# The last expert's mask of remaining rows in the second mixture's search: made and read in PSUM instead of SBUF

## The chip, the core and the metric

The kernel runs on one core of one Trainium2 chip. The metric is the device time of one execution in microseconds (us), the median over several runs. TensorE (PE) multiplies matrices out of SBUF into PSUM; VectorE (DVE), ScalarE (ACT) and GpSimd (POOL) do elementwise work; SyncE (SP) issues most DMAs. Each engine runs its own instructions in order and waits on semaphores of the others. DVE and ACT reach SBUF and PSUM, POOL reaches SBUF.

## What is computed

Causal attention with a decay (4 batches, 8 heads, 576 positions, 64 wide) gives 2304 rows of 512. Two mixtures of experts follow. The change lies in the second, whose reference is:

```python
def _moe2_ref(x, w_gate, w1, w2):
    N, D = x.shape                 # 2304, 512
    E = w_gate.shape[1]            # 8
    cap = N // E                   # 288
    logits = x @ w_gate
    order = np.argsort(-logits.flatten())
    assigned = -np.ones(N, dtype=np.int64)
    counts = np.zeros(E, dtype=np.int64)
    for idx in order:
        tok, e = (int(idx) // E, int(idx) % E)
        if assigned[tok] >= 0 or counts[e] >= cap:
            continue
        assigned[tok] = e
        counts[e] += 1
    out = np.zeros((N, D), dtype=np.float32)
    for e in range(E):
        mask = assigned == e
        out[mask] = np.maximum(x[mask] @ w1[e], 0.0) @ w2[e]
    return out
```

Row after row takes the best expert that still has room; every expert ends with 288 rows.

## The kernel before

**The second mixture** (`Moe2Quick`) fills one expert after the other, in phases 0 to 7. For each phase `search` finds the expert and the threshold, `hand` makes the mask `m` of that expert's rows (tile `mem`) and reads the expert's number to SP, which can then fetch its weights; `listing` turns the mask into row numbers (two groups of matmuls, L1927 to L1929 and the 21 of L1954, with DVE work between) and gathers the rows with three indirect DMAs on POOL; `prep` transposes the gathered rows; and `FFN.run` does the expert's two layers. Rows are kept 128 to a partition, 18 columns (`NT`); `V` holds the 8 logits of each row (18 x 8 on the free axis), large negative where the row or the expert is closed.

**The last phase (ph = 7) has no threshold.** All rows not yet taken belong to it. In `search` (L1804 to L1811) `es` becomes a mask of the one open expert, L1807 takes the maximum of each row's 8 logits, L1808 turns it into 1 (row open) or 0, and `hand` uses this mask as `new`: L1903 and L1905 find the rows whose first choice is that expert among those of earlier phases, and L1907 adds `new`. The mask is a tile `v` of the SBUF pool `p`. The other phases keep such small results in PSUM: `open` (L1775 to L1778) takes one bank for the search and names its columns:

```python
S, G = self.S, self.G = [self.ps.tile([128, 512], F32, name=n) for n in ("sq", "gq")]
self.base, self.u, self.g = S[:, 96:128], S[:, 128:128 + NT], S[:, 152:152 + NT]
self.hg = S[:, 208:208 + NT * E].rearrange("p (t e) -> p t e", e=E)
```

so that `u`, the maximum of each row, is 18 columns of the tile that the profile calls `sq`. Phases 1 to 6 write it at L1814; nothing reads it after phase 6.

**An expert's two layers.** `FFN.run` makes 8 groups (f = 0 to 7) of 12 matmuls at L733: four pieces of the contraction, three products each, since every factor is split into a rounded part (`xh`, `wh`) and a rest (`xl`, `wl`). A group's result lies in one of four PSUM tiles `ph`. ACT writes its rounded positive part (`hh`, L761; `h`, L764), and DVE the rest of it (`hl`, L737, called `low`). Only after `low` is the PSUM tile free, so group f needs `low` of group f - 4, or of a tile used before. `by_row` (L799, L806) does the second layer. The weights come in 8 pieces of 512 KB per expert: SP issues the DMA into `wraw` (L685, L689), ACT rounds it into `wh` (L699), POOL subtracts into `wl` (L703, 128 x 1024). POOL also issues the gathers (L1968) and, three per expert, the scatters of finished rows (L2037).

**The order of the work.** A schedule is built as the program is written: generators ("lanes" for search, listing, prep and out) yield the time at which a model of the engines (`pace`) expects their next step to be ready, and are woven between the matmuls of `run`. Each engine then keeps that order. So DVE has the `low` of groups 1 and 2 behind the whole of `hand(7)`.

Of the kernel before, what the change touches and what calls it, by code (L numbers as in the profile page):

```python
# [7 lines left out]
F32 = mybir.dt.float32  # L8
# [4 lines left out]
ALU = mybir.AluOpType  # L13
AX = mybir.AxisListType
# [1259 lines left out]
class Moe2:  # L1274
# [7 lines left out]
    NT = N // 128  # L1282
# [343 lines left out]
class Moe2Quick(Moe2):  # L1626
# [158 lines left out]
    def search(self):  # L1785

        nc, p, NT, rt, pace = self.nc, self.p, self.NT, self.rt, self.f.pace
        V, rem, S, es, u, g, acc, base = self.V, self.rem, self.S, self.es, self.u, self.g, self.acc, self.base
# [12 lines left out]
        for ph in range(E):  # L1801
            while ph > self.cur + 2:
                yield pace.t + 1.0
            if ph == E - 1:  # L1804
                nc.vector.tensor_scalar(es, rem, 1e8, None, op0=ALU.is_lt)
                op = p.tile([128, NT], F32, name="v")
                nc.vector.tensor_reduce(op, V, axis=AX.X, op=ALU.max)  # L1807
                nc.vector.tensor_scalar(op, op, -1.0, None, op0=ALU.is_gt)  # L1808
                pace.dve(0.8)
                self.hand(ph, es, op)  # L1810
                return  # L1811
            hb, thr = self.hb0, self.thr
            if ph:
# [6 lines left out]
                                               op0=ALU.mult, op1=ALU.add, accum_out=room)  # L1820
# [382 lines left out]
```

## Time and profile before

| | |
|---|---|
| Runs of the kernel | median 766.86 us of 3 (765.68 to 766.95) |
| The profiled execution | 765.09 us, of which 763.4 us from the first to the last instruction (the span) |
| PE busy | 692.2 us (91%), granted clock 0.952 on average |
| DVE, ACT, POOL busy | 349.1 us (46%), 393.8 us (52%), 488.2 us (64%) |
| Second mixture, expert phase 4: first L733 to the next expert's | 629.71 to 660.71 us |
| The same, phase 5 | 660.71 to 698.01 us |

Times in views are us from the span's start. A row of a timeline gives start, duration, engine, line, operation, the tile written and those read, their shapes, and in brackets how long the engine sat idle before and what released it. The granted clock is the share of TensorE's full speed (2.4 GHz) that the chip's throttle let through, so 0.50 is 1.2 GHz. DVE's instructions in a timeline may overlap a little, because the next one starts while the last one drains; the step from start to start is then the better measure.

### The profile page before, as it was taken

The numbers are of one execution on the slowest core, as the hardware profiler recorded it, in microseconds if no ns is written. First come the engines' busy times: TensorE is split into PE (matmuls) and PEld (weight loads), VectorE is DVE, ScalarE is ACT, GpSimd is POOL, SyncE is SP. The second block draws the span as 40 slices with busy tenths as digits, with TensorE's granted clock in tenths as the row PEclk, the third lists the DMA queues.
The fourth block names the chain that finished last, engine by engine and source line by source line (L and its number), as shares of the span: only waits on it lengthen the run. The fifth ranks groups of instructions, "written<-read, shape, count | busy, mean of one in ns | idle before, by whom it ended". The sixth has DMA issues, their size and how long they took to land. (4 is left out here: it accounts for less than half of the span.)

```text
span 763.4 us, 16041 instructions
## 1 busy us (share of the span) xinstructions
PE 692.2 (91%) x5723; PEld 576.1 (75%) x5723; DVE 349.1 (46%) x1307; ACT 393.8 (52%) x924; POOL 488.2 (64%) x524
## 2 busy tenths in 40 slices
PE   6999999999529999999999998399999999979994
PEld 3566565665329999999999987287878989868893
DVE  4776675866622222232232243655636646472120
ACT  5988788787115455455555551143533535434440
POOL 6666338170248676777777872359779788768861
PEclk9999999999759999999999999579999999989997
DMA  6588556220168272743835800347527366268201
GB/s 199 170 315 304 187 177 215 86 102 2 63 216 286 84 253 75 268 157 138 294 117 178 279 33 28 91 166 252 190 94 248 125 195 210 90 214 278 62 34 39
DMA packets 79395, 124.32 MB, mean 163 GB/s; under 512 B 10989, under 2 KB 43757, under 8 KB 79296
## 3 DMA queue, kind: packets, MB, share of 16 engines
q1 hardware_dynamic: 72944, 103.80, 41.4%
q0 software_dynamic: 6160, 18.97, 6.8%
q8 instruction: 49, 0.80, 0.4%
q14 instruction: 50, 0.41, 0.2%
q10 hardware_dynamic: 192, 0.34, 0.1%
HBM read 101.08 MB, written 22.18 MB: 161 GB/s over the span
## 5 line engine op out<-in xcount | busy, mean ns | idle before, releaser
L703 POOL TENSOR_TENSOR wl<-wraw,wh 128x1024 fp32r<-128x1024 f32 x128 | 305.4, 2397 | 100.2 <-ACT wh L699 94.7
L733 PE MATMUL ph<-xh,wh 128*128 128x288 f32 (+6 forms) x512 | 162.8, 318 | 5.7 <-DVE hl L737 4.3
L733 PE MATMUL ph<-xl,wh 128*128 128x288 f32 (+6 forms) x512 | 155.3, 303 | 0.6 <-DVE xl L2004 0.3
L699 ACT CAST wh<-wraw 128x1024 fp32r<-128x1024 f32 x128 | 132.7, 1050 | 44.6 <-DMA wraw<-in_moe_w_dram 31.7
L733 PE MATMUL ph<-xh,wl 128*128 128x288 f32 (+6 forms) x512 | 154.5, 302 | 0.0
L761 ACT ACTIVATE hh<-ph 128x256 fp32r<-128x256 f32 (+6 forms) x128 | 51.5, 402 | 112.7 <-PE ph L733 107.4
L733 PEld LDWEIGHTS ph<-xh,wh 128*128 128x128 f32 x512 | 99.2, 194 | 10.7 <-issue 8.0
L733 PEld LDWEIGHTS ph<-xl,wh 128*128 128x128 f32 x512 | 99.2, 194 | 2.0 <-DVE xl L2004 1.8
L737 DVE SCALAR_TENSOR_TENSOR hl<-ph,hh 128x256 fp32r<-128x256 f32 (+6 forms) x128 | 55.6, 442 | 96.5 <-ACT hh L761 55.8
L733 PEld LDWEIGHTS ph<-xh,wl 128*128 128x128 f32 x512 | 98.8, 193 | 0.2 <-POOL wl L703 0.2
L174 ACT ACTIVATE z<-z,mx 128x128 f32<-128x128 f32 (+2 forms) x144 | 84.0, 584 | 27.1 <-DVE mx L177 25.2
L177 DVE CUSTOM_DVE_ANT_0 z<-ps,cx 128x128 f32<-128x128 f32 (+2 forms) x144 | 68.6, 518 | 51.0 <-PE ps L188 33.5
L733 PE MATMUL ph<-hh,wh 128*128 128x288 f32 (+6 forms) x256 | 79.4, 310 | 0.0
L733 PE MATMUL ph<-hh,wl 128*128 128x288 f32 (+6 forms) x256 | 76.8, 300 | 0.9 <-POOL wl L703 0.8
L733 PE MATMUL ph<-hl,wh 128*128 128x288 f32 (+6 forms) x256 | 76.7, 300 | 0.0
L151 POOL TENSOR_SCALAR_AFFINE_SELECT cx<-cb 128x256 f32<-128x256 f32 (+1 forms) x64 | 44.5, 726 | 38.9 <-DVE mx L177 16.9
L208 ACT COPY pt<-tp 128x512 f32<-128x512 f32 (+2 forms) x128 | 49.9, 438 | 7.3 <-PE tp L216 5.8
L799 PE MATMUL ph<-wh,hh 128*128 128x512 f32 x128 | 53.6, 419 | 0.0
L799 PE MATMUL ph<-wh,hl 128*128 128x512 f32 x128 | 50.6, 395 | 0.0
L216 PEld LDWEIGHTS tp<-ident,z 128*128 128x128 f32 x320 | 34.7, 140 | 20.7 <-ACT z L174 6.9
L799 PE MATMUL ph<-wl,hh 128*128 128x512 f32 x128 | 50.3, 393 | 0.0
L733 PEld LDWEIGHTS ph<-hh,wl 128*128 128x128 f32 x256 | 48.3, 189 | 1.4 <-POOL wl L703 1.4
(353 smaller groups left out, 1192.2 us busy)
## 6 DMA issues: line engine op xcount, KB each, us to landing
wraw<-in_moe_w_dram SPq DMA_DIRECT2D x128, 512.0 KB
cb<-c8d SPq DMA_DIRECT2D x15, 576.0 KB
xs<-zrow SPq DMA_DIRECT2D x8, 803.1 KB
xg<-xs SPq DMA_DIRECT2D x6, 771.0 KB
kd<-in_k_dram SPq DMA_DIRECT2D x16, 288.0 KB
qd<-in_q_dram SPq DMA_DIRECT2D x16, 288.0 KB
vt<-in_v_dram SPq DMA_DIRECT2D x4, 1024.0 KB
x<-zrow SPq DMA_DIRECT2D x1, 1080.0 KB
```

The lines of the kernel that those rows point to most:

```text
L151: nc.gpsimd.affine_select(cx[:, :, CB0[i]:CB0[i] + w], cb[:, :, :w], pattern=[[0, 2], [-1, w]], compare_op=ALU.is_ge, fill=-8e9, base=128 ...
L174: nc.scalar.activation(z, z, AF.Exp, bias=mx[:, c:c + 1], scale=-1.0, accum_out=sm[:, c:c + 1])
L177: nc.vector.tensor_tensor_reduce(out=z, in0=p, in1=cx, scale=-0.125, scalar=3e38, op0=ALU.add, op1=ALU.min, accum_out=mx[:, c:c + 1])
L208: self.nc.scalar.copy(o, i)
L216: nc.tensor.transpose(o, z[:, CB0[i] + 128 * kb:CB0[i] + 128 * kb + 128], self.ident)
L699: nc.scalar.copy(wh, t)
L703: nc.gpsimd.tensor_sub(wl[:, q], t[:, q], wh.bitcast(F32)[:, q])
L733: mm = lambda o, w, m, st, sp: nc.tensor.matmul(o, lhsT=w, rhs=m, start=st, stop=sp)
L737: nc.vector.scalar_tensor_tensor(out=hl[:, :W], in0=p[:, :W], scalar=0.0, in1=hh.bitcast(F32)[:, :W], op0=ALU.max, op1=ALU.subtract)
L761: nc.scalar.activation(hh[:, :W], p[:, :W], AF.Relu)
L799: mm = lambda o, w, m, st, sp: nc.tensor.matmul(o, lhsT=w, rhs=m, start=st, stop=sp)
```

## The change

The mask of the last phase is no longer a tile of its own in SBUF. L1807 writes the maximum into `u`, the 18 PSUM columns of `sq`, L1808 compares in place there, and `hand` gets `u`:

```diff
             if ph == E - 1:
                 nc.vector.tensor_scalar(es, rem, 1e8, None, op0=ALU.is_lt)
-                op = p.tile([128, NT], F32, name="v")
-                nc.vector.tensor_reduce(op, V, axis=AX.X, op=ALU.max)
-                nc.vector.tensor_scalar(op, op, -1.0, None, op0=ALU.is_gt)
+                nc.vector.tensor_reduce(u, V, axis=AX.X, op=ALU.max)
+                nc.vector.tensor_scalar(u, u, -1.0, None, op0=ALU.is_gt)
                 pace.dve(0.8)
-                self.hand(ph, es, op)
+                self.hand(ph, es, u)
                 return
```

Every engine has as many instructions as before and in the same order; in the lines below the tile statement the numbers fall by one. L1807, L1808 and L1907 name `sq` where they named `v`. The SBUF tile's writes and reads on DVE carried one wait, of L1808 on L1807; in its place L1807 waits for the DVE instruction ahead of it, L1808 for L1807, and L1903, which also reads `sq`, for L1808, all on DVE's own semaphore. Below, lines are given by the numbers of the kernel before.

## Rows read from the trace of the kernel before

**Rows 1.** PE's waits, 660 to 698 us: reader, releaser, us in total, times, longest.
```profile
PE ph L733 <- DVE hl L737: 4.3, 1, 4.3
PE gq L1927 <- DVE spl L1971: 0.6, 1, 0.6
```

**Rows 2.** PE's timeline, 668 to 691 us: start, us, instruction, idle before and releaser.
```profile
668.08 0.29 PE L733 MATMUL ph<-xh,wh 128*128 128x288 f32 x1
...
669.54 0.29 PE L733 MATMUL ph<-xh,wl 128*128 128x288 f32 x1
674.18 0.58 PE L733 MATMUL ph<-xh,wh 128*128 128x288 f32 x1 [4.35 <-DVE hl L737]
674.56 0.44 PE L733 MATMUL ph<-xl,wh 128*128 128x288 f32 x1
...
679.36 0.34 PE L733 MATMUL ph<-xh,wh 128*128 128x288 f32 x1
...
680.20 0.70 PE L1954 MATMUL gq<-ht,lbw 128*128 128x24 bf16 x21
...
690.93 0.60 PE L1997 MATMUL tq<-ident,xg 128*128 128x128 f32 x4
```

**Rows 3.** Stretches: PE, PEld, DVE, ACT, POOL busy (x), granted clock, DMA, GB/s.
```profile
673.00:674.00 1.00, 0.00 (x0) 0.00 (x0) 0.96 (x6) 0.00 (x0) 0.39 (x1) 0.50 1.06 374
...
681.00:682.00 1.00, 0.54 (x6) 0.53 (x6) 0.78 (x6) 0.00 (x0) 0.70 (x2) 1.00 0.03 10
```

**Rows 4.** DVE's timeline around the last phase's mask, 667 to 677 us.
```profile
667.68 0.29 DVE L1807 TENSOR_REDUCE v<-V 128x18 f32<-128x144 f32 x1
668.01 1.87 DVE L1808 TENSOR_SCALAR v<-v 128x18 f32<-128x18 f32 x1
669.79 0.29 DVE L1903 TENSOR_TENSOR ae<-AQ,sq 128x144 bf16<-128x144 bf16 x1
...
670.45 2.98 DVE L1907 TENSOR_TENSOR mem<-mem,v 128x18 bf16<-128x18 bf16 x1
673.36 0.15 DVE L1910 CUSTOM_DVE_ANT_0 ev<-sq,ie 128x8 f32<-128x8 f32 x1
...
673.62 0.75 DVE L737 SCALAR_TENSOR_TENSOR hl<-ph,hh 128x256 fp32r<-128x256 f32 x2
...
676.84 0.75 DVE L737 SCALAR_TENSOR_TENSOR hl<-ph,hh 128x256 fp32r<-128x256 f32 x2
```

**Rows 5.** POOL's timeline in the same place, 667 to 679 us.
```profile
667.41 2.42 POOL L703 TENSOR_TENSOR wl<-wraw,wh 128x1024 fp32r<-128x1024 f32 x1
...
670.02 0.99 POOL L2037 DMA_INDIRECT out_dram<-yl,idx  x1 [0.19 <-issue]
671.04 2.35 POOL L703 TENSOR_TENSOR wl<-wraw,wh 128x1024 fp32r<-128x1024 f32 x1
678.92 2.39 POOL L703 TENSOR_TENSOR wl<-wraw,wh 128x1024 fp32r<-128x1024 f32 x1 [5.53 <-ACT wh L699]
```

**Rows 6.** POOL's timeline in phase 1 of the search, 506 to 526 us.
```profile
506.75 18.90 POOL L703 TENSOR_TENSOR wl<-wraw,wh 128x1024 fp32r<-128x1024 f32 x8 [8.92 <-ACT wh L699]
```

**Rows 7.** DVE's timeline within that stretch, 513 to 518 us.
```profile
513.21 0.30 DVE L1902 TENSOR_TENSOR AQ<-AQ,sq 128x144 bf16<-128x144 bf16 x1
...
514.30 0.15 DVE L1913 CAST ei<-el 128x1 int32<-128x1 f32 x1
...
515.12 0.31 DVE L1814 TENSOR_REDUCE sq<-V 128x18 f32<-128x144 f32 x1
...
517.27 0.18 DVE L1936 TENSOR_SCALAR gq<-gq 128x18 int32<-128x18 int32 x1
517.49 0.18 DVE L1937 TENSOR_SCALAR gq<-gq 128x18 int32<-128x18 int32 x1
```

**Rows 8.** DVE's timeline near the end, 739 to 741 us.
```profile
739.85 1.26 DVE L2093 COPY slots<-idx 128x2 int32<-128x2 int32 x1
```

**Rows 9.** POOL's timeline in the same place, 736 to 741 us.
```profile
736.33 4.75 POOL L703 TENSOR_TENSOR wl<-wraw,wh 128x1024 fp32r<-128x1024 f32 x2
```

## The prediction

> **What bounds the kernel now.** I read PE's waits first, for the stretch of expert phase 5, because the changed lines run there. PE is the busiest engine, and in this stretch it waits only twice: 4.3 us at L733 for DVE's `hl`, and 0.6 us later [rows 1]. PE's timeline shows the long one as one gap. A group's matmuls start every 0.133 us up to 669.54 (eleven steps in 1.46 us from 668.08); the next should start at 669.67 and starts at 674.18 [rows 2]. That matmul opens group 5 and needs the PSUM tile that `low` of group 1 has to release. So the question is what kept DVE.
>
> DVE's timeline answers it. `low` of groups 1 and 2 stands at 673.62, right behind `hand(7)`, and in front of it two instructions on 18 columns take very long: L1808 1.87 us, L1907 2.98 us [rows 4]. POOL's timeline beside them: the subtract at L703 runs from 667.41 to 669.83, and L1808 ends at 669.88; an indirect DMA from 670.02 and the next subtract, 671.04 to 673.39, cover L1907, which ends at 673.43 [rows 5]. L1808 has its source and result in SBUF, L1907 both its inputs. The neighbours in the same place are not held: L1807 took 0.29 us inside the first subtract.
>
> Is it POOL, and is it the place of the operands? Two comparisons say so. Near the end a copy of two SBUF columns takes 1.26 us and ends at 741.11 [rows 8], just after POOL's pair of subtracts at 741.08 [rows 9]. And while POOL subtracts without a break from 506.75 to 525.65 [rows 6], the hand-over of phase 1 goes through at 0.15 to 0.31 us an instruction: tensor by tensor with one input in PSUM (L1902), a maximum into PSUM (L1814, the twin of the new L1807), comparisons and shifts within PSUM (L1936, L1937) [rows 7].
>
> A second cost hangs on the gap. PE stood still from 669.83, the end of a matmul at full rate, and in 673 to 674 us the granted clock is 0.50 [rows 3], that is 1.2 GHz instead of 2.4. From 674.56 matmuls start every 0.24 us (twenty steps in 4.80 us), until 679.36, where the short spacing returns [rows 2].
>
> **The change, part by part.**
>
> L1807 writes PSUM instead of SBUF: 0.31 us by L1814 [rows 7] against 0.29 [rows 4], 0.02 us more. Its new wait on the DVE instruction ahead costs nothing I can see: L1814 stands behind DVE work too. I keep L1808's start at 668.01 plus 0.02 = 668.03.
>
> L1808, now within PSUM: the nearest is L1936, 18 columns, with 0.22 us to the next start (517.27 to 517.49, and L1937 waits for L1936 as L1903 now waits for L1808) [rows 7]. Before, the step to L1903 was 1.78 us [rows 4]. Gain 1.56 us.
>
> L1907, one input now in PSUM: L1902 has these types and places, 0.30 us for 144 columns [rows 7]; for 18 I take 0.22 us to the next start, as for L1936. Before it was 673.36 - 670.45 = 2.91 us [rows 4]. Gain 2.69 us.
>
> Sum on DVE: 1.56 + 2.69 - 0.02 = 4.23 us. `low` then starts at 673.62 - 4.23 = 669.39. PE began 0.56 us after it (674.18 - 673.62), so now at 669.95, 0.28 us after the 669.67 at which it could. The stall is all but gone and **4.23 us** are won on PE.
>
> With a pause of 0.28 us instead of 4.5 I expect no fall of the clock. Between 674.18 and L1954 at 680.20 stand 27 matmuls of L733, in 6.02 us [rows 2]. At full clock they take 27 x 0.133 = 3.59, plus 0.1 for the start after a pause: 3.69. Gain **2.33 us**. Together 6.56, say **6.6 us**.
>
> What is late next? Group 7 needs `low` of group 3, at 676.84 on DVE [rows 4], moved to 672.61; PE could use it at 673.17, and reaches group 7 after 24 matmuls, at 669.95 + 3.19 + 0.1 = 673.24. That is just in time; if not, it costs 0.1 us. The 0.6 us wait for `spl` [rows 1] stays: DVE there waits for PE's own matmuls. POOL moves less than PE: its next subtract, idle 5.53 us before 678.92 [rows 5], can start no earlier than the last one ends, 673.39, which is 5.5 us earlier against 6.6. Behind it stand three gathers of the kind at 670.02, about 1.3 us each with the gap. Before, these were issued by 678.92 + 2.39 + 3.9 = 685.2, and PE first reads gathered rows at 690.93 [rows 2]. That margin of 5.7 us shrinks by 1.1, and covers it. SP reads the expert's number off `hand(7)` and only moves earlier with it.
>
> The Trainium skill speaks against the change: "VectorE: DVE Perf Modes", in its section on the TRN2 errata, gives DVE a fixed 58 cycles from SBUF and 120 from PSUM, and calls the faster mode of a comparison SBUF-only. By that table alone the two instructions would get 0.14 us longer (an estimate from its figures), and the time would be 767.0. The rows show the same sign, 0.02 us, for a maximum, and next to 1.87 and 2.98 us it is small.
>
> **The time.** The profiled execution took 765.09 us, so it would take 758.5. It is 1.8 below the median of 766.86, and the runs reach from 765.68 to 766.95. A run without this stall would be 6.6 lower, and none is, so all runs have it. From the median I get **760.3 us**.
>
> **The rivals.**
>
> A cast held in the place of the mask: L1913 goes from SBUF to SBUF, and in the new timing it falls at about 669.3, inside the subtract that ends at 669.83. Held until then, `low` starts 0.5 us later: gain 6.1, 760.8 us. Against it: L1913 took 0.15 us at 514.30 [rows 7], with POOL subtracting all the while [rows 6]. The Trainium skill, "SBUF — State Buffer", section on who interferes with whom, lets a cast enter the two-port mode that shuts out GpSimd, if its shape allows; this trace's cast of one column was not held. Chance 0.08.
>
> The clock falls all the same, because two pauses and the 21 small matmuls of L1954 lie close together: only 4.2 are won, 762.6 us. For it speaks the new pause of 0.28 and the 0.6 that stays; against it that the clock before was 1.00 in 681 to 682 us, which holds the 0.6 us wait and comes right behind those small matmuls [rows 3]. Chance 0.06.
>
> POOL becomes the bound, as its chain moves by 5.5 only: 761.4 us. The margin above speaks against it. Chance 0.04.
>
> The change does not do what it says: the long durations come from something other than the operands' place (L1907's hold began under an indirect DMA, and no other row here shows a hold under one), and both stay. Then 766.9. Chance 0.06.
>
> Slower: the clock falls later and stays down through phase 5's second layer. Its 48 products of 512 columns (three per row tile and piece) take about twice as long at 1.2 GHz; a 288-column matmul loses 0.107 us [rows 2], one of 512 columns, by its width, 0.19 us, so all 48 lose 9.1. Net 9.1 - 6.6 = 2.5 us slower, 769.4. It decides from 35 such matmuls on. Against it: before, the clock was back at 1.00 just ahead of that layer, after a far longer pause [rows 3]. Chance 0.04.
>
> **How the numbers follow.** The forecast has 0.72. About 0.2%, 1.5 us, is what a measurement of this kernel can tell from no change. The forecast and the first three rivals are all faster by more: 0.90. No change 0.06, slower 0.04. The range leaves out only these last 0.10: upward to the clock rival from the highest run, 766.95 - 4.2 = 762.8; downward to the profiled execution less 7.1 (the stall gone whole, 4.51, plus 2.33, plus part of the 0.6), 758.0.
>
> **What would show it.** In the changed kernel's profile: L1808 and L1907 at 0.15 to 0.25 us while POOL subtracts; `low` of groups 1 and 2 within 2 us after L1807; PE's wait at L733 for `hl` under 0.5 us; granted clock 1.00 through 669 to 685 us; phase 5 from first L733 to the next expert's at about 30.7 us instead of 37.3. The forecast is wrong if one of the two stays above 1 us, if L1913 is the long one, or if PE's waits in phases 5 to 7 grow elsewhere by microseconds.

## The result and the profile after

The changed kernel takes 758.78 us, the median of 6 runs (758.49 to 760.37), against 766.27 us of 6 runs of the kernel before (765.04 to 767.65). The ratio is 0.9906, 95% interval 0.9891 to 0.9920: 7.2 us faster, between 6.1 and 8.4 (the medians themselves are 7.5 us apart). The prediction was 760.3 us (758.0 to 762.8) and 6.6 us faster. The profiled executions took 765.09 and 758.66 us, with spans of 763.4 and 757.0.

Below the tile statement that was taken away, line numbers are one lower than before: L1808 is now L1807, L1907 is L1906. DVE's timeline of the changed kernel in the place of [rows 4] (start, us, instruction):

```profile
667.39 0.17 DVE L1805 TENSOR_SCALAR sq<-rem 128x8 f32<-128x8 f32 x1
667.59 0.31 DVE L1806 TENSOR_REDUCE sq<-V 128x18 f32<-128x144 f32 x1
667.94 0.18 DVE L1807 TENSOR_SCALAR sq<-sq 128x18 f32<-128x18 f32 x1
668.15 0.30 DVE L1902 TENSOR_TENSOR ae<-AQ,sq 128x144 bf16<-128x144 bf16 x1
668.49 0.30 DVE L1904 TENSOR_REDUCE mem<-ae 128x18 bf16<-128x144 bf16 x1
668.83 0.17 DVE L1906 TENSOR_TENSOR mem<-mem,sq 128x18 bf16<-128x18 bf16 x1
668.92 0.16 DVE L1909 CUSTOM_DVE_ANT_0 ev<-sq,ie 128x8 f32<-128x8 f32 x1
...
669.12 0.15 DVE L1912 CAST ei<-el 128x1 int32<-128x1 f32 x1
669.19 0.74 DVE L737 SCALAR_TENSOR_TENSOR hl<-ph,hh 128x256 fp32r<-128x256 f32 x2
```

The two long instructions are short: 1.87 became 0.18 us, 2.98 became 0.17. POOL's first subtract and its indirect DMA stand as before; of the two subtracts behind them, the later one no longer comes after 5.53 us of idling but at once. This is POOL's timeline in the place of [rows 5]:

```profile
667.23 2.42 POOL L703 TENSOR_TENSOR wl<-wraw,wh 128x1024 fp32r<-128x1024 f32 x1
...
669.85 0.99 POOL L2036 DMA_INDIRECT out_dram<-yl,idx  x1 [0.17 <-issue]
670.86 4.75 POOL L703 TENSOR_TENSOR wl<-wraw,wh 128x1024 fp32r<-128x1024 f32 x2
675.77 1.05 POOL L1967 DMA_INDIRECT xg<-x,idx  x1 [0.16 <-DVE gq L1935]
```

All of the mask's instructions run inside the subtract of 667.23 to 669.65, the cast L1912 too, and none is held. Two of them, the reduction L1904 and the cast L1912, have all their tensors in SBUF. PE's timeline, in the place of [rows 2], has no pause marked any more:

```profile
669.33 0.29 PE L733 MATMUL ph<-xh,wl 128*128 128x288 f32 x1
669.75 0.37 PE L733 MATMUL ph<-xh,wh 128*128 128x288 f32 x1
669.96 0.30 PE L733 MATMUL ph<-xl,wh 128*128 128x288 f32 x1
...
673.42 0.70 PE L1953 MATMUL gq<-ht,lbw 128*128 128x24 bf16 x21
...
684.15 0.60 PE L1996 MATMUL tq<-ident,xg 128*128 128x128 f32 x4
```

From the last matmul of group 4 to the first of group 5 it is 0.42 us instead of 0.133, so 0.29 us are lost where 4.5 were. From there to the small matmuls of the listing it takes 3.67 us (669.75 to 673.42) instead of 6.02. PE's waits from 655 to 700 us, in the place of [rows 1]:

```profile
PE gq L1926 <- DVE spl L1970: 0.6, 1, 0.6
PE tq L1996 <- DVE xl L2003: 0.5, 1, 0.5
```

The second is the pause of phase 6's preparation, which the kernel before has too (0.51 us at 703.62 in its PE timeline, put down to the issue there). The stretches of that place, in the columns of [rows 3]:

```profile
668.00:670.00 2.00, 1.87 (x15) 1.66 (x14) 1.86 (x10) 1.75 (x5) 1.83 (x3) 1.00 0.80 260
670.00:672.00 2.00, 2.00 (x17) 2.00 (x17) 1.83 (x8) 0.51 (x5) 1.98 (x2) 1.00 1.04 317
672.00:674.00 2.00, 2.00 (x33) 1.93 (x33) 1.48 (x4) 1.50 (x5) 2.00 (x2) 1.00 0.82 267
```

The granted clock stays at 1.00. Phase 5, from its first L733 to that of phase 6, goes from 660.52 to 691.23: 30.71 us instead of 37.30. The rest of the span is nearly what it was: 0.2 us less ahead of phase 5, 0.4 us more behind it.

### The profile page after: what moved, and what is told of

Read it like the earlier page. It is cut to its first block, busy times and chain, and to the rows that moved or that the text cites. A ratio compares the mean times of both kernels' runs of the same rounds, so it can differ in the third digit from the quotient of the medians.

```text
span 757.0 us, 16041 instructions
## 1 busy us (share of the span) xinstructions
PE 688.1 (91%) x5723; PEld 572.3 (76%) x5723; DVE 344.8 (46%) x1307; ACT 393.6 (52%) x924; POOL 488.3 (65%) x524
## 5 line engine op out<-in xcount | busy, mean ns | idle before, releaser
L733 PE MATMUL ph<-xh,wh 128*128 128x288 f32 (+6 forms) x512 | 161.1, 315 | 1.4 <-ACT xh L2009 0.7
L733 PE MATMUL ph<-xl,wh 128*128 128x288 f32 (+6 forms) x512 | 154.0, 301 | 0.6 <-DVE xl L2003 0.3
L733 PE MATMUL ph<-xh,wl 128*128 128x288 f32 (+6 forms) x512 | 153.1, 299 | 0.0
L733 PEld LDWEIGHTS ph<-xh,wh 128*128 128x128 f32 x512 | 97.7, 191 | 6.4 <-issue 3.4
L733 PEld LDWEIGHTS ph<-xl,wh 128*128 128x128 f32 x512 | 97.7, 191 | 2.0 <-DVE xl L2003 1.7
L733 PEld LDWEIGHTS ph<-xh,wl 128*128 128x128 f32 x512 | 97.6, 191 | 0.2 <-POOL wl L703 0.2
L733 PE MATMUL ph<-hh,wh 128*128 128x288 f32 (+6 forms) x256 | 79.4, 310 | 0.0
L733 PE MATMUL ph<-hh,wl 128*128 128x288 f32 (+6 forms) x256 | 76.8, 300 | 0.9 <-POOL wl L703 0.8
L733 PE MATMUL ph<-hl,wh 128*128 128x288 f32 (+6 forms) x256 | 76.7, 300 | 0.0
L733 PEld LDWEIGHTS ph<-hh,wl 128*128 128x128 f32 x256 | 48.3, 189 | 1.4 <-POOL wl L703 1.4
```

The costliest lines, as they stand in the source:

```text
L733: mm = lambda o, w, m, st, sp: nc.tensor.matmul(o, lhsT=w, rhs=m, start=st, stop=sp)
```

## Experiments

My theory had three links: POOL's subtract holds the comparison and the addition when all their tensors are in SBUF (not every instruction of that kind: the maximum L1807 before, from `V` to `v`, took 0.29 us inside a subtract, and the reduction and the cast above were not held either); PE stands still because `low` is queued behind; the clock falls because PE stands still. The rivals: the two instructions are slow for another reason; the indirect DMA holds the addition; the clock falls for POOL's or the DMAs' sake; the order on DVE, and not the place of the mask, is what counts. The sharpest measure is the length of phase 5 in each kernel's profile (first L733 to first L733), one execution each, beside the ratio of the runs. The ratios are to runs of the kernel before at the same time: median 766.27 us for the change, 766.77 for the next four kernels, 766.87 for the last three.

| kernel | runs, us | ratio to the kernel before (95%) | phase 5, us |
|---|---|---|---|
| before | | | 37.30 |
| the change | 758.78 | 0.9906 (0.9891 to 0.9920) | 30.71 |
| read_in_sbuf | 760.98 | 0.9928 (0.9905 to 0.9950) | 31.39 |
| made_in_sbuf | 761.92 | 0.9938 (0.9915 to 0.9961) | 32.49 |
| no_subtract | 760.99 | 0.9924 (0.9904 to 0.9945) | 30.43 |
| delay_4us | 766.86 | 0.9997 (0.9983 to 1.0011) | 36.93 |
| delay_3us | 762.57 | 0.9946 (0.9928 to 0.9964) | 36.41 |
| later_in_sbuf | 758.94 | 0.9905 (0.9889 to 0.9921) | 30.40 |
| later_in_psum | 759.42 | 0.9907 (0.9892 to 0.9922) | 30.53 |

### Each instruction alone back in SBUF

First only the addition reads SBUF, made from the changed kernel:

```diff
+                op = p.tile([128, NT], F32, name="v")
                 nc.vector.tensor_reduce(u, V, axis=AX.X, op=ALU.max)
-                nc.vector.tensor_scalar(u, u, -1.0, None, op0=ALU.is_gt)
+                nc.vector.tensor_scalar(op, u, -1.0, None, op0=ALU.is_gt)
                 pace.dve(0.8)
-                self.hand(ph, es, u)
+                self.hand(ph, es, op)
```

> The maximum stays in PSUM, but the comparison writes its result to SBUF, so that only the addition to the mask has both inputs in SBUF. Theory (a POOL subtract holds a DVE instruction whose tensors are all in SBUF): comparison 0.2 us; the addition starts about 1.2 us after the maximum, inside the subtract that ended at 669.65 in the changed kernel, and ends with it: 0.9 us, low 0.8 us later, PE pause about 1.1 us, time 759.6 against 758.8 of the changed kernel. If it misses the moment between two POOL instructions it stays held to the end of the next subtract: 4.4 us, time 765 to 766. Rival (the addition was held only because an indirect DMA ran): 0.2 us, 758.8.

DVE's timeline of this kernel (its line numbers are those of the kernel before):

```profile
669.14 0.18 DVE L1808 TENSOR_SCALAR v<-sq 128x18 f32<-128x18 f32 x1
...
669.90 0.98 DVE L1907 TENSOR_TENSOR mem<-mem,v 128x18 bf16<-128x18 bf16 x1
```

and POOL's:

```profile
668.41 2.42 POOL L703 TENSOR_TENSOR wl<-wraw,wh 128x1024 fp32r<-128x1024 f32 x1
670.75 0.09 POOL L2030 MEMSET sp<- 1x1 f32 x1
671.02 0.99 POOL L2037 DMA_INDIRECT out_dram<-yl,idx  x1 [0.18 <-issue]
```

The comparison, from PSUM into SBUF, is not held. The addition is, to 670.88, just after the subtract's end at 670.83, and it gets in ahead of the next DMA. No indirect DMA ran when it began. PE waited 0.80 us where I expected 1.1, the clock stayed at 1.00, and phase 5 is 0.68 us longer than in the changed kernel. The runs took 760.98 us where I expected 759.6; their interval overlaps that of the change, so the cost of this hold is read from phase 5 and not from them.

Then the comparison alone, in SBUF, with a copy of its result to PSUM:

```diff
+                op = p.tile([128, NT], F32, name="v")
-                nc.vector.tensor_reduce(u, V, axis=AX.X, op=ALU.max)
-                nc.vector.tensor_scalar(u, u, -1.0, None, op0=ALU.is_gt)
+                nc.vector.tensor_reduce(op, V, axis=AX.X, op=ALU.max)
+                nc.vector.tensor_scalar(op, op, -1.0, None, op0=ALU.is_gt)
+                nc.vector.tensor_copy(u, op)
                 pace.dve(0.8)
                 self.hand(ph, es, u)
```

> Maximum and comparison in SBUF as before, then a copy to PSUM, so that the addition has one input in PSUM. Theory: comparison held to the end of the subtract, 1.7 us; copy and addition 0.2 us each; low about 1.8 us later than in the changed kernel, PE pause 2.1 us, no fall of the clock: 760.6. If the clock falls with it: 762 to 763. Rival (the comparison's long time is not a hold by POOL): 759.

DVE's timeline (line numbers one higher than before):

```profile
669.04 1.89 DVE L1808 TENSOR_SCALAR v<-v 128x18 f32<-128x18 f32 x1
670.96 0.18 DVE L1809 COPY sq<-v 128x18 f32<-128x18 f32 x1
...
671.85 0.17 DVE L1908 TENSOR_TENSOR mem<-mem,sq 128x18 bf16<-128x18 bf16 x1
```

and POOL's:

```profile
668.46 2.42 POOL L703 TENSOR_TENSOR wl<-wraw,wh 128x1024 fp32r<-128x1024 f32 x1
```

The subtract ended at 670.88, the comparison at 670.93. PE waited 1.90 us with the clock at 1.00, and phase 5 is 1.78 us longer than in the changed kernel, near the 1.8 expected. The runs took 761.92 us, 1.3 above the expected 760.6. So each of the two is held by itself, and by phase 5 each alone costs about its own length. Together they cost 6.6 us in the kernel before, because the second was held through an indirect DMA and a second subtract, and the clock fell.

### The subtracts away, the mask in SBUF

```diff
+            if self.by_rows and s in (45, 46):
+                nc.scalar.mul(wl[:, q], wh.bitcast(F32)[:, q], 0.0)
+                continue
             nc.gpsimd.tensor_sub(wl[:, q], t[:, q], wh.bitcast(F32)[:, q])
```

> The kernel before, mask in SBUF, but the two subtracts beside it are not there: for two of the 64 weight pieces ScalarE writes zeros in place of the rest (this leaves out two rest products of one expert). Theory: comparison and addition 0.1 to 0.3 us each, PE pause under 0.6 us, 758.5 to 760; up to 1 us more for each of the two that an indirect DMA holds. Rival (the two instructions are slow for another reason): still 1.9 and 3.0 us, 766.

DVE's timeline (line numbers three higher than before):

```profile
669.19 0.18 DVE L1811 TENSOR_SCALAR v<-v 128x18 f32<-128x18 f32 x1
...
669.95 0.18 DVE L1910 TENSOR_TENSOR mem<-mem,v 128x18 bf16<-128x18 bf16 x1
```

and POOL's:

```profile
668.89 0.97 POOL L2040 DMA_INDIRECT out_dram<-yl,idx  x1 [0.23 <-issue]
```

Both take 0.18 us with all their tensors in SBUF. The comparison fell into an indirect DMA of POOL (668.89 to 669.86) and was not held by it; the addition met an idle POOL. That settles the first link for these two instructions: it takes the subtract to make them long. The runs came out 1 us above the expected 758.5 to 760; the interval overlaps that of the change, and phase 5 is 0.3 us shorter.

### The pause without the hold

```diff
                 nc.vector.tensor_scalar(u, u, -1.0, None, op0=ALU.is_gt)
+                for _ in range(19):
+                    nc.vector.tensor_scalar(u, u, 1.0, None, op0=ALU.mult)
```

> The changed kernel with 19 more DVE instructions on the mask in PSUM (a multiplication by 1), 0.22 us each, 4.2 us in all, which POOL cannot hold. Theory (PE's pause and the clock that falls with it are all that the holds cost): PE pause 4.4 us, granted clock 0.50 after it, 758.8 + 4.2 + 2.3 = 765.3. Rival (the fall of the clock, or a part of the loss, comes from POOL's work or the DMAs in that place and not from the pause): 763.0.

PE's waits from 655 to 700 us in this kernel, in the columns of [rows 1]:

```profile
PE ph L733 <- DVE hl L737: 4.3, 1, 4.3
PE gq L1928 <- DVE spl L1972: 0.6, 1, 0.6
```

and two stretches, in the columns of [rows 3]:

```profile
674.00:676.00 2.00, 0.47 (x2) 0.50 (x3) 1.86 (x10) 0.00 (x0) 0.84 (x1) 0.50 0.97 323
676.00:678.00 2.00, 2.00 (x10) 2.00 (x9) 1.86 (x7) 0.00 (x0) 0.00 (x0) 0.50 0.41 122
```

The loss is back: 766.86 us, ratio 0.9997, with PE's pause at 4.29 us and the granted clock at 0.50 from 674 to 680 us. DVE work that POOL does not touch does the same as the holds. In phase 5 it is 6.22 us of the 6.59. I had expected 765.3, on the changed kernel's median; the rest lies, by the profile, ahead of phase 5, which begins at 662.15 us here and at 660.52 in the changed kernel.

With 14 instructions:

> The changed kernel with 14 more DVE instructions on the mask in PSUM, 3.1 us. PE pause 3.2 us. Pauses of 0.8 and 1.9 us left the granted clock at 1.00, one of 4.3 us halved it. If the loss is proportional to the pause: 758.8 + 3.1 and some clock, 763 to 764. If the clock falls whole or not at all: 764.2 or 761.9, and the granted clock shows 0.50 or 1.00 behind the pause.

PE waited 3.19 us, and in the profiled execution the clock fell to 0.50 (674 to 680 us), with phase 5 at 36.41 us. But the five runs differ: 761.27, 762.10 and 762.57 us with a mean clock of 0.958 to 0.960, and 764.74 and 766.06 with 0.954 and 0.952. They look like the two outcomes I named, whole or not at all, both in one program. That is not shown: only the run of 766.06 us was profiled, and the kernel before has means from 0.952 to 0.960 among its own runs of that time. The sums speak for it. If the fastest run had the profiled phase 5 (36.41 us) and the profiled 65.6 us behind it, its span of 759.6 us would leave 657.6 us ahead of phase 5, where the traces of this kernel and of the three others traced beside it have 660.6 to 662.4.

### Who stands behind the hold

The kernel before, mask in SBUF, but the hand-over is issued later in the schedule:

```diff
             if ph == E - 1:
+                yield pace.t + 5.5
                 nc.vector.tensor_scalar(es, rem, 1e8, None, op0=ALU.is_lt)
```

> The kernel before, mask in SBUF, but the last phase's hand-over is issued 5.5 us later in the schedule, so that low of groups 1 to 4 stands ahead of it on DVE. Theory (the holds cost what waits behind them): still two long instructions, but PE no longer waits at L733 for hl; it waits up to 2 us for the mask at the listing matmuls or for low of group 5, no fall of the clock: 759.5 to 761.5. Rival (the mask in SBUF costs the same wherever it stands): 766.

DVE's timeline (line numbers one higher than before):

```profile
667.41 0.75 DVE L737 SCALAR_TENSOR_TENSOR hl<-ph,hh 128x256 fp32r<-128x256 f32 x2
...
670.62 0.75 DVE L737 SCALAR_TENSOR_TENSOR hl<-ph,hh 128x256 fp32r<-128x256 f32 x2
...
671.68 1.77 DVE L1809 TENSOR_SCALAR v<-v 128x18 f32<-128x18 f32 x1
...
674.03 0.18 DVE L1908 TENSOR_TENSOR mem<-mem,v 128x18 bf16<-128x18 bf16 x1
```

The comparison is still held, for 1.77 us, to the end of a subtract that ran from 670.98 to 673.41, but four `low` are ahead of it, and PE waits nowhere at L733. The addition met an idle POOL, so one hold is left of the two that I expected. The time is that of the change, 758.94 us, ratio 0.9905. I expected 759.5 to 761.5, with up to 2 us of waiting at the listing; it was 0.53, against 0.56 in the changed kernel. So the hold of the comparison costs what is queued behind it, and this schedule does as well as PSUM.

And the changed kernel with `low` of group 1 ahead (1.5 us in the same line):

> The changed kernel, with low of group 1 issued ahead of the last phase's hand-over on DVE. Theory: the rest of PE's pause before group 5 goes too, 0.2 to 0.3 us, too little to be told from the changed kernel: 758.5, ratio to the kernel before 0.990. Rival (order matters more than the holds): 757 or less.

759.42 us, ratio 0.9907. The last 0.29 us of pause went (phase 5 30.53 against 30.71), and the runs can't tell it. No version beat the change by what a measurement can show.

### What held the addition while only a DMA ran

One thing in [rows 4, 5] did not fit: the addition was held from 670.45, when POOL's indirect DMA was running and no subtract. I moved the DMA with memsets, in the kernel without the two subtracts:

```diff
+            if t == 2 and self.cur == 5:
+                for _ in range(7):
+                    self.nc.gpsimd.memset(self.sp1, 0.0)
             self.nc.gpsimd.memset(self.sp1, 0.0)
```

> The kernel without the two subtracts (mask in SBUF, two rest products left out), and POOL's third indirect DMA of that place pushed back by seven empty memsets, 0.6 to 0.7 us, so that the addition to the mask falls inside it. If an indirect DMA holds an addition with both inputs in SBUF, as the kernel before seemed to show from 670.45 to 671.01, the addition takes 0.5 us or more and ends with the DMA's instruction. If only the subtracts hold, it takes 0.18 us as without the shift; then the addition of the kernel before must have lost its turn to the next subtract in another way.

It overshot: the addition (0.18 us at 669.39) ended before the DMA began at 669.79, so this run says nothing on it. With three memsets:

> As the kernel with the indirect DMA pushed back, but by three memsets instead of seven, which overshot (the addition came 0.4 us ahead of the DMA). The addition should now begin inside the DMA's instruction. If an indirect DMA holds an addition with both inputs in SBUF: 0.4 us or more, to the end of the DMA's instruction. If only subtracts hold: 0.18 us.

DVE's timeline of that kernel, and under it POOL's:

```profile
669.21 0.18 DVE L1910 TENSOR_TENSOR mem<-mem,v 128x18 bf16<-128x18 bf16 x1
```

```profile
669.02 0.97 POOL L2043 DMA_INDIRECT out_dram<-yl,idx  x1 [0.66 <-PE ph L736]
```

The addition ran inside the DMA's instruction and was not held.

> The same with two memsets, in case three put the DMA too late. If an indirect DMA holds the addition: 0.3 us or more, to the end of the DMA's instruction; if only subtracts hold: 0.18 us.

The same two timelines:

```profile
671.33 0.18 DVE L1910 TENSOR_TENSOR mem<-mem,v 128x18 bf16<-128x18 bf16 x1
```

```profile
671.01 0.97 POOL L2043 DMA_INDIRECT out_dram<-yl,idx  x1 [0.66 <-PE ph L736]
```

Here the addition began at 671.33 inside a DMA from 671.01 to 671.98, and took 0.18 us again. So the DMA is not it. What the kernel before had, and these two not, is a subtract ready behind the DMA: its `wh` was rounded by 669.69. I put that subtract back, with the DMA and the addition moved so that they meet:

> The addition with both inputs in SBUF again begins inside an indirect DMA's instruction, but now POOL has a subtract ready right behind it, as in the kernel before at 670.45 (one of the two subtracts is back; one rest product is left out; eleven memsets push the DMA back, and six DVE instructions in PSUM push the addition back by 1.3 us). If the subtract that waits behind the DMA holds the addition before it has begun: about 3 us, to the subtract's end. If it holds only while it runs: 0.18 us, and the hold of the kernel before stays unexplained in its first 0.56 us.

DVE's timeline, POOL's, and ACT's cast of the weights that this subtract waits for:

```profile
668.67 3.06 DVE L1912 TENSOR_TENSOR mem<-mem,v 128x18 bf16<-128x18 bf16 x1
```

```profile
668.35 0.97 POOL L2045 DMA_INDIRECT out_dram<-yl,idx  x1 [0.66 <-issue]
669.34 2.35 POOL L706 TENSOR_TENSOR wl<-wraw,wh 128x1024 fp32r<-128x1024 f32 x1
```

```profile
667.25 1.05 ACT L699 CAST wh<-wraw 128x1024 fp32r<-128x1024 f32 x1
```

The cast ended at 668.30, the addition began at 668.67 under the DMA, the subtract ran from 669.34 to 671.69, and the addition ended at 671.73.

> The same with nine memsets, so that the addition comes later within the DMA's instruction. The same two outcomes: about 2.5 to 3 us to the subtract's end, or 0.18 us.

The same, by DVE's timeline and POOL's:

```profile
667.80 2.77 DVE L1912 TENSOR_TENSOR mem<-mem,v 128x18 bf16<-128x18 bf16 x1
```

```profile
667.18 0.98 POOL L2045 DMA_INDIRECT out_dram<-yl,idx  x1 [0.66 <-issue]
668.16 2.37 POOL L706 TENSOR_TENSOR wl<-wraw,wh 128x1024 fp32r<-128x1024 f32 x1
```

The addition ended at 670.57, the subtract at 670.53. A subtract that is ready behind a running POOL instruction holds the addition before it has begun itself.

## Why the prediction was right

**The holds.** I took 0.22 us from start to start for each of the two instructions. The comparison has 0.21 (667.94 to 668.15), though its stand-in L1936 is a shift: I wrote that [rows 7] hold comparisons within PSUM, and they hold none. The addition has 0.09 (668.83 to 668.92), 0.13 less than I took. From the maximum's start to `low` it is 1.60 us instead of 5.94, 4.34 us less. The maximum itself starts later, though. I put its new wait at nothing, and it shows: from L1805's start to the maximum's it was 0.08 us (667.60 to 667.68) and is 0.20 (667.39 to 667.59). So `low` comes 4.22 us earlier after L1805, where I had 4.23. That the two agree so closely is luck: one step was 0.13 too long and one 0.12 too short. The row of L1805 before the change:

```profile
667.60 0.17 DVE L1805 TENSOR_SCALAR sq<-rem 128x8 f32<-128x8 f32 x1
```

**PE's pause** before group 5 is 0.29 us where I had 0.28, and the clock stayed. From group 5's start to the listing's small matmuls it is 3.67 us, where I had 3.69; the 0.1 us in it for the start after a pause, for which I named no row, measures 0.08 (669.75 to 669.96, less 0.133). The sum of 6.56 stands against 37.30 - 30.71 = 6.59 in phase 5.

**What is late next.** `low` of group 3 came in time, and PE did not wait for it. POOL's gathers of phase 6 start at 675.77, and PE reads gathered rows at 684.15 without waiting for the gathers, so the margin that I had for POOL's smaller shift held. POOL subtracts without a break from 670.86 to 675.61, and from the end of the gathers to that first read it is 4.70 us (679.45 to 684.15) where it was 5.64 (685.29 to 690.93): 0.94 us less, where I had 1.1.

**The rivals.** The cast L1912 ran at 669.12, inside the subtract, in 0.15 us: not held. The Trainium skill ("SBUF — State Buffer", section on who interferes with whom) lets a cast take both ports only where its shape allows; this trace's cast of one column agrees. The clock did not fall, POOL is not the bound, and nothing got slower. Against the page of the Trainium skill that spoke for a loss ("VectorE: DVE Perf Modes", the section on the TRN2 errata; that the faster mode of a comparison is for SBUF alone stands in its section on why PSUM operands drop a tier), the unheld comparison takes 0.18 us in SBUF (no_subtract), 0.18 from PSUM into SBUF (read_in_sbuf) and 0.18 in PSUM, the addition 0.18 with both inputs in SBUF and 0.17 with one in PSUM: the longer time for PSUM does not show in these durations, and the measurement decides.

**Where it was a little off.** The time is 1.5 us below the forecast: 0.6 because the six runs of the kernel before have their median at 766.27 us and not at the 766.86 that I started from, 0.9 because the medians are 7.5 apart and not 6.6. In the profiles the gain is 765.09 - 758.66 = 6.4 us, and phase 5 alone gives 6.59. The profiled execution of the kernel before, at 765.09 us, lay 1.2 us below the median of its six runs, which is about the rest. Where executions differ, the traces of all the kernels here tell: phase 5 begins between 658.43 and 663.27 us, though the code ahead of it is the same, and what follows phase 5 takes 65.3 to 65.9 us in each. So the spread arises ahead of the changed place; from 200 to 300 us, for one, the granted clock is 0.86 to 0.90 from trace to trace. What causes it is open.

## What to carry to other kernels

A DVE comparison or addition of 18 columns can last 3 us when all it touches lies in SBUF and POOL has a subtract of SBUF tensors running, or ready behind the instruction that runs; a maximum, a reduction and a one-column cast in SBUF were not held. One PSUM operand in its place freed it, and the price here was one wait of 0.12 us. Look for instructions whose duration is out of proportion to their size, and end with a POOL instruction, then ask what stands behind them in the queue: in later_in_sbuf a hold of 1.77 us cost nothing, here two of 4.5 us cost 6.6, because PE's PSUM tiles were freed behind them and the clock fell in the pause.

## What was not expected of the hardware

A subtract that only waits its turn on POOL already holds DVE: 3.06 and 2.77 us where the indirect DMA ahead of it, without a subtract behind, held nothing (0.18 us twice). And the cost of a pause on PE is not proportional to its length. In the profiles with pauses of 0.80 and 1.90 us the granted clock stayed at 1.00 and phase 5 grew by 0.68 and 1.78 us; with 3.19 and 4.29 us the clock fell to 0.50 and phase 5 grew by 5.70 and 6.22 us. Behind pauses of 3.77 and 4.04 us (subtract_queued9, subtract_queued) it is 0.50 too. At 3.19 us the runs of one program lie up to 4.8 us apart; that some of them kept the clock is likely from the sums above, and not shown.
